# A delta-rule attention and two-MoE kernel: 32-row inverse steps on VectorE and GpSimd for the first two units, and a reordered start

## The chip, the cores and the metric

The kernel runs on 1 core of one Trainium2 chip. The metric is the device time of one execution in microseconds (us), lower is better. The engines are TensorE (PE in the profile; its weight loads are PEld), VectorE (DVE), ScalarE (ACT), GpSimd (POOL) and SyncE (SP), which issues most DMAs.

## The reference

Three stages follow each other. The first is a delta-rule attention over 4 x 8 heads, 768 tokens, head dimension 48; its output is laid out as 3072 tokens of 384 numbers. The second is a mixture of 8 experts of width 1024 whose weights P come from a softmax-like matrix that is normalised 8 times by rows and columns. The third is a dense layer of width 2048 with h * cos(h) in the middle.

```python
k_n = k / (norm(k) + 1e-06)
for t in range(S):
    y[:, :, t] = q[:, :, t] @ state
    v_old = k_n[:, :, t] @ state
    state = state + beta[t] * outer(k_n[:, :, t], v[:, :, t] - v_old)
...
logits = x @ w_gate; P = exp(logits - logits.max())
for _ in range(8):
    P /= P.sum(1) + 1e-09; P /= P.sum(0) + 1e-09; P *= N / E
for e in range(E):
    out += P[:, e:e + 1] * (maximum(x @ w1[e], 0.0) @ w2[e])
...
h = x @ w_in
return (h * cos(h)) @ w_out
```

## The kernel before, in words

The attention runs in 12 units of 64 tokens (C = 64), each split into two blocks of 32 (CB = 32). A unit holds all 32 heads as 16 systems side by side (NS = 16) in 4 groups of 32 partitions. Inside a block the recurrence is a unit lower triangular system, and the kernel inverts it: N is the triangular matrix of key products times beta (tiles n0 and ns0 of the buffer scr for units 0 and 1, Nst and Nsys for two units at a time later), transposed by VectorE so that each system lies in one partition as 32 x 32. The inverse is then built by a ladder of steps j: a product (row j of the result times column j) into a temporary, and an addition into all rows below j. Each step needs the one before it.

- For units 2 and 3 and later pairs the ladder (inv_ops, lines 388 and 392) runs on GpSimd over 32 rows: 30 steps of two instructions. It starts with the transpose into Nsys on VectorE (L374) and an affine_select on GpSimd (L377) into Xsys, a part of the buffer w1t.
- For units 0 and 1 the ladder (inv16, lines 408 and 409) runs on VectorE as two 16-row blocks at once: 14 steps of two instructions, on data whose upper triangles have been set to zero by a product with the mask m16 (L824). The off-diagonal 16 x 16 block is made on TensorE afterwards by merge16_a (L418), a scaling on VectorE (L427) and merge16_b (L437), then added by merge16_c (L444) and transposed (L447).
- The inverse comes out in two orientations, tiles tx and dm. pe_Z1 (L463) and pe_Z2 (L475) combine the two 32-token blocks of a unit into the tile Bs; pe_U multiplies it with the values (L526), and VectorE takes the product out of PSUM into U (L532). pe_S (L541, L546) updates the state, pe_PU (L556) and pe_XT (L573) make the unit's output.

The order of the work at the start is written out by hand, call by call, under manual_schedule, and each engine executes its instructions in that order. The string SEQ follows: its letters are read by tick (U pe_U, S pe_S, P pe_PU, K and k the products with the state, Z or Y and z or y the two halves of Bs, X the output transpose, H the first expert's first matmuls (L139), m half a step of the first expert, a and b the splitting of its weights, r and R the transposes of the later inverse into dm and tx). From H on, the expert matmuls of L139 and L150 are mixed in between the attention units, and then follow the other experts and the last layer.

The tick function calls inv_some(3) before every letter, which takes up to three queued ladder steps; before the change the queue is already empty when SEQ starts, since inv_some(99) has issued all of it to GpSimd.

norm_a and norm_b compute key norms for a pair of units, norm_pe (L783) swaps them across partitions on TensorE, beta_raw (L791, L795) folds them into beta, and n_dve (L807, then a product on GpSimd, L345) completes N for units 2 and 3. go_beta (L771) scales the tile Go that pe_Z1 reads, v_scale (L239) scales V, and pp_mask (L829) masks the tile Pp on GpSimd.

Of the kernel before, what the change touches and what calls it, by code (L numbers as in the profile page):

```python
# [11 lines left out]
ALU = mybir.AluOpType  # L12
# [13 lines left out]
SEQ = ("U0 a0 y1 o2 S0 x1 b0 P0 K1 o3 k1 v U1 X0 P1 S1 X1 H0 x2",  # L26
# [12 lines left out]
def kernel(  # L39
# [133 lines left out]
    m16 = ap1.tile([128, CB], F32, name="m16")  # L173
# [4 lines left out]
    betam = ap1.tile([128, 2, NS], F32, name="betam")  # L178
# [193 lines left out]
    def inv_ops(nst, nsys, xsys, tmp, eng):  # L372

        ops = [lambda: nc.vector.transpose(out=nsys, in_=nst.rearrange("p s t -> p t s"))]  # L374

        def first():
            nc.gpsimd.affine_select(  # L377
                out=xsys, in_=nsys, pattern=[[1, CB], [-1, CB]], compare_op=ALU.is_gt, fill=0.0, base=0,
                channel_multiplier=0,
            )  # L380
            nc.gpsimd.memset(xsys.rearrange("p t i -> p (t i)")[:, 0:CB * CB:CB + 1], 1.0)

        ops.append(first)
# [12 lines left out]
        return ops


    def inv16(xsys, tmp):
# [4 lines left out]
        def step(j):
            n = 15 - j
            a = tmp[:, 0:2 * n * j].rearrange("p (a t i) -> p a t i", a=2, t=n)
            x = blk(j + 1, 0, CB, 1, n, j)
            nc.vector.tensor_tensor(out=a, in0=blk(j + 1, j, CB, 0, n, j), in1=blk(j, 0, 0, 1, n, j), op=ALU.mult)
            nc.vector.tensor_tensor(out=x, in0=x, in1=a, op=ALU.add)

        return [lambda j=j: step(j) for j in range(1, 15)]

    def merge16_a(u, n, bank, y=True):

# [7 lines left out]
        if y:  # L422
            merge16_y(u, bank)

    def merge16_y(u, bank):
        ym[u] = ap2.tile([128, NS, CB], F32, tag="W", name="ym")
        nc.vector.tensor_tensor(  # L427
            out=ym[u][:, :, 0:16], in0=bank[:, 0:NS * 16].rearrange("p (s t) -> p s t", t=16),
            in1=betam[:, u, :, None].to_broadcast([128, NS, 16]), op=ALU.mult,
        )  # L430

    def merge16_b(u, bank, s0=0, s1=NS):
        y = ym[u]
        for s in range(s0, s1):
            for p in range(4):
                r = slice(p * CB, p * CB + CB)
                nc.tensor.matmul(  # L437
                    out=bank[r, (NS + s) * 16:(NS + s + 1) * 16], lhsT=dm[r, u * NS + s, :], rhs=y[r, s, 0:16],
                    start=True, stop=True, skip_group_check=True,
                )  # L440
# [8 lines left out]
    ym = {}  # L449
# [20 lines left out]
    def pe_Z2(u, bank=pcd[:, 1]):  # L470
# [8 lines left out]
        if u not in Bs:  # L479
            bs_act(u)  # L480
# [8 lines left out]
    def bs_act(u):  # L489
        x = tx[:, (u % 2) * NS:(u % 2 + 1) * NS, :]  # L490
        Bs[u] = ap2.tile([128, NS, C], F32, tag="Bs", name="Bs", bufs=1)
        for a in range(2):
            nc.scalar.activation(out=Bs[u][:, :, a * CB:a * CB + CB], in_=x, func=ACTF.Copy, scale=hm[:, a:a + 1])
# [204 lines left out]
    with tc.manual_schedule():  # L698
# [34 lines left out]
        nc.gpsimd.memset(m16, 1.0)  # L733
        nc.gpsimd.memset(hm, 0.0)
        for r in range(4):
            m = m16[r * CB:(r + 1) * CB]
            nc.gpsimd.affine_select(
                out=m, in_=m, pattern=[[1, CB]], compare_op=ALU.is_gt, fill=0.0, base=0, channel_multiplier=-1
            )
            nc.gpsimd.memset(m[0:16, 16:CB], 0.0)  # L740
# [3 lines left out]
            nc.gpsimd.memset(h_[0:16, 4:5], 1.0)  # L744
# [11 lines left out]
        inv_q = []  # L756

# [30 lines left out]
        def beta_raw(u0, bank):  # L788
# [6 lines left out]
            nc.vector.tensor_copy(out=dv[:, u0:u0 + 2, :].rearrange("p u (m i) -> p u m i", i=2), in_=x[:, 1])  # L795
# [62 lines left out]
        nc.vector.transpose(out=ns0, in_=xs0.rearrange("p s t -> p t s"))  # L858
# [11 lines left out]
        for u in range(2):  # L870
            nc.scalar.activation(
                out=betam[:, u].rearrange("p (i m) -> p i m", i=2),
                in_=beta_sb[:, u, 0:NS].rearrange("p (m i) -> p i m", i=2), func=ACTF.Copy, scale=hm[:, 4:5],
            )
# [7 lines left out]
        n_act(3, p23)  # L882
        pe_GQ_mms(1, p01)
# [61 lines left out]
        def tick(u, seq):  # L945
            early = u < 2
            for x, c in enumerate(seq.split()):
# [983 lines left out]
```

## Time and profile before

| what | value |
|---|---|
| median of 3 runs | 2084.89 us (2082.3 to 2086.13) |
| the profiled execution | 2088.02 us |
| its span, first to last instruction | 2085.9 us |
| PE busy | 2053.4 us, 98% of the span |
| PEld busy | 1729.9 us, 83% |
| DVE busy | 1461.4 us, 70% |
| ACT busy | 866.1 us, 42% |
| POOL busy | 905.7 us, 43% |
| mean granted TensorE clock | 0.987 |

Busy times are of one profiled execution; the shares of the engines overlap. An engine's busy share is an average over stages with different limits, so the stage that a change touches has to be read by itself: here the first hundred microseconds.

### The profile page before, as it was taken

What the parts mean: (1) busy time and instruction counts of PE and PEld (TensorE: products, weight loads), DVE (VectorE), ACT (ScalarE), POOL (GpSimd) and SP (SyncE); (2) the same over time, 40 slices, a digit from 0 to 9 for tenths busy, and PEclk for the clock granted to TensorE, in tenths of its full rate; (3) what the DMA queues carried; (4) which work ended last, traced back from release to release, by engine and by line L of the source; (5) the groups of instructions that cost most, each with busy time, mean ns of one, the idle gap of its engine ahead of it and who ended that gap; (6) DMA issues with size and microseconds to landing.
All of it is one profiled execution on the core that took longest, in us unless ns stands there. A gap on an engine that the chain in (4) does not pass through costs nothing.

```text
span 2085.9 us, 39694 instructions
## 1 busy us (share of the span) xinstructions
PE 2053.4 (98%) x16132; PEld 1729.9 (83%) x16132; DVE 1461.4 (70%) x2253; ACT 866.1 (42%) x1436; POOL 905.7 (43%) x1012
## 2 busy tenths in 40 slices
PE   7999999999999999999999999999999999999999
PEld 6887888778888888888888888888888889999998
DVE  6665537677677777777767787787788666666665
ACT  3442333344444444434333333333333356666664
POOL 4676660156555655544353333333333343333331
PEclk7899999999999999999999999999999999999999
DMA  5532346765554544453684544535354551011000
GB/s 94 127 94 57 78 127 196 296 237 164 193 172 157 204 169 169 177 179 136 249 302 143 173 151 142 173 120 192 130 174 144 185 201 31 1 31 31 16 16 15
DMA packets 212470, 294.39 MB, mean 141 GB/s; under 512 B 86160, under 2 KB 159344, under 8 KB 212288
## 3 DMA queue, kind: packets, MB, share of 16 engines
q1 hardware_dynamic: 208368, 284.20, 41.3%
q0 software_dynamic: 1664, 6.49, 0.9%
q8 instruction: 126, 2.06, 0.4%
q10 hardware_dynamic: 2256, 1.18, 0.2%
q14 instruction: 56, 0.46, 0.1%
HBM read 188.95 MB, written 113.87 MB: 145 GB/s over the span
## 4 chain that ended last, share of the span: by engine, by line
PE 91%; POOL 3%; DVE 2%; SPq 1%; issue 1%; DMA 1%; ACT 1%; ACTq 0%; POOLq 0%; DVEq 0%
PE ps L150 36%; PE ps L1469 27%; PE ps L1759 10%; PE ps L1717 9%; PE ps L139 4%; PE ps L313 1%; POOL w1t L392 1%; POOL w1t L388 1%; PE ps L498 1%; PE ps L281 1%; PE ps L526 1%; PE ps L463 0%; PE ps L556 0%; PE ps L475 0%; PE ps L573 0%
## 5 line engine op out<-in xcount | busy, mean ns | idle before, releaser
L150 PE MATMUL ps<-mh,w2t 128*128 128x512 f32 x3060 | 749.3, 389 | 0.4 <-DVE cth L1505 0.4
L150 PEld LDWEIGHTS ps<-mh,w2t 128*128 128x128 f32 x3060 | 573.5, 188 | 122.0 <-DVE cth L1505 3.3
L1469 PE MATMUL ps<-T,w1t 128*128 128x512 f32 x2520 | 627.2, 389 | 1.9 <-ACT ct L1474 0.8
L1506 POOL TENSOR_TENSOR accp<-accp,cth 128x512 f32<-128x512 f32 x246 | 320.3, 1333 | 562.8 <-DVE cth L1505 562.8
L1469 PEld LDWEIGHTS ps<-T,w1t 128*128 128x128 f32 x2520 | 472.2, 188 | 101.6 <-ACT ct L1474 1.3
L156 ACT ACTIVATE mh<-ps 128x512 fp32r<-128x512 f32 x340 | 203.6, 600 | 620.7 <-PE ps L1469 237.3
L157 DVE SCALAR_TENSOR_TENSOR mh<-ps,mh 128x512 fp32r<-128x512 f32 x340 | 228.8, 688 | 176.8 <-ACT mh L156 175.4
L1474 ACT ACTIVATE scr<-ps 128x512 f32<-128x512 f32 x224 | 134.5, 600 | 163.7 <-PE ps L1469 154.4
L1726 POOL TENSOR_SCALAR tp<-tp 128x512 f32<-128x512 f32 x92 | 91.5, 994 | 204.2 <-ACT tp L1725 204.2
L1505 DVE TENSOR_TENSOR cth<-ps,scr 128x512 f32<-128x512 f32 x246 | 154.3, 684 | 15.2 <-PE ps L150 13.3
L1740 DVE TENSOR_TENSOR tp<-tp,ps 128x512 f32<-128x512 f32 x96 | 66.1, 688 | 133.5 <-ACT tp L1739 133.5
L1477 DVE TENSOR_TENSOR ps<-scr,ps 128x512 f32<-128x512 f32 x168 | 116.5, 694 | 54.6 <-PE ps L1469 53.1
L139 PE MATMUL ps<-xb,w1t 128*128 128x512 f32 (+1 forms) x441 | 111.4, 397 | 0.0
L150 PE MATMUL ps<-h,w2t 128*128 128x512 f32 x396 | 100.8, 400 | 0.0
L1477 DVE TENSOR_TENSOR scr<-ps,scr 128x512 f32<-128x512 f32 x112 | 77.1, 689 | 30.5 <-PE ps L1469 29.2
L139 PEld LDWEIGHTS ps<-xb,w1t 128*128 128x128 f32 x441 | 78.6, 188 | 17.1 <-DVE xb L579 0.9
L1309 DVE TENSOR_TENSOR w1t<-wraw,w1t 128x512 fp32r<-128x512 f32 (+2 forms) x81 | 74.7, 934 | 19.1 <-ACT w1t L1306 17.9
L150 PEld LDWEIGHTS ps<-h,w2t 128*128 128x128 f32 x396 | 73.4, 190 | 15.7 <-issue 0.2
L392 POOL TENSOR_TENSOR w1t<-w1t 128x30 f32<-128x30 f32 (+9 forms) x150 | 80.7, 538 | 11.7
L1717 PE MATMUL ps<-xx,cw 128*128 128x512 f32 x360 | 84.0, 390 | 0.0
L388 POOL TENSOR_TENSOR w1t<-Nsys,w1t 128x30 f32<-128x30 f32 (+9 forms) x150 | 77.9, 520 | 11.4
L1725 ACT ACTIVATE tp<-ps 128x512 f32<-128x512 f32 x96 | 56.2, 586 | 63.5 <-PE ps L1717 63.5
(286 smaller groups left out, 2769.2 us busy)
## 6 DMA issues: line engine op xcount, KB each, us to landing
wss<-w1t SPq DMA_DIRECT2D x56, 768.0 KB
w1t<-wss SPq DMA_DIRECT2D x56, 768.0 KB
w2t<-w2c SPq DMA_DIRECT2D x56, 384.0 KB
T<-tsc SPq DMA_DIRECT2D x22, 512.0 KB
scr<-pts SPq DMA_DIRECT2D x44, 256.0 KB
w2c<-in_moe_w_dram SPq DMA_DIRECT2D x28, 384.0 KB
wss<-w1t SPq DMA_DIRECT2D x28, 384.0 KB
w1t<-wss SPq DMA_DIRECT2D x28, 384.0 KB
```

The lines of the kernel that those rows point to most:

```text
L139: nc.tensor.matmul(out=ps[:, :nn], lhsT=w[:, a, kk, fs], rhs=x[:, b, kk, c0:c0 + nn], start=(i == 0), stop=(i == 3 * KD - 1),)
L150: nc.tensor.matmul(out=banks[kd], lhsT=w[:, a, f % 2, kd * 128:(kd + 1) * 128], rhs=h[:, b, :], start=(first and b == 0 and a == 0), stop= ...
L156: nc.scalar.activation(out=h[:, 0, :nn], in_=ps[:, :nn], func=ACTF.Relu)
L157: nc.vector.scalar_tensor_tensor(out=h[:, 1, :nn], in0=ps[:, :nn], scalar=0.0, in1=h[:, 0, :nn].bitcast(F32), op0=ALU.max, op1=ALU.subtract,)
L392: eng.tensor_tensor(out=xsys[:, j + 1:, 0:j], in0=xsys[:, j + 1:, 0:j], in1=a, op=ALU.add)
L1469: nc.tensor.matmul(out=bank, lhsT=s_of(n, nm, a), rhs=T[:, b, :], start=start and q == 0, stop=q == 2, skip_group_check=True)
L1474: nc.scalar.activation(out=out, in_=in_, func=ACTF.Copy, scale=scale)
L1477: nc.vector.tensor_tensor(out=out, in0=a, in1=b, op=op)
L1505: nc.vector.tensor_tensor(out=c, in0=yb[kd], in1=pslot[t], op=ALU.mult)
L1506: nc.gpsimd.tensor_tensor(out=a[:, kd, :], in0=a[:, kd, :], in1=c, op=ALU.add)
L1717: nc.tensor.matmul(out=hb2(i), lhsT=net_w1(f, a, kk), rhs=x2[b](c, kk), start=(j == 0), stop=(j == 3 * KD - 1))
L1759: nc.tensor.matmul(out=ybk[t][:, :DM], lhsT=h[:, a, ts], rhs=net_w2(f, c), start=(f == 0 and j == 0), stop=(f == FT2 - 1 and j == 2),)
```

## The change

Units 0 and 1 get a 32-row ladder that is split over two engines. VectorE runs steps 1 to 15 on columns 0 to 15 of all rows (step 15 only on rows 16 to 23), GpSimd runs the 16-row ladder of the lower right block and step 15 on rows 24 to 31. What was above the diagonal is cleared by 12 memsets on GpSimd (upper_zero) in place of the products with m16, and one of the two TensorE passes of the merge goes away. Scalings by beta and the mask of Pp for unit 1 move to GpSimd (go_beta, pp_mask); norms and the products of units 2 and 3 keep their place relative to them. Further, inv_ops gets an argument last: from step 22 on the steps of the first later pair (units 2 and 3) are issued to VectorE. Of the 32 queued operations all but 8 are issued at the start, and the last 8 wait in inv_last until letter r. pe_U(0), pe_Z1(1) and pe_S(0) move from SEQ into the start.

```diff
-SEQ = ("U0 a0 y1 o2 S0 x1 b0 P0 K1 o3 k1 v U1 X0 P1 S1 X1 H0 x2",
+SEQ = ("P0 y1 a0 x1 K1 b0 o2 k1 o3 v U1 X0 P1 S1 X1 H0 x2",
...
-    def inv_ops(nst, nsys, xsys, tmp, eng):
+    def inv_ops(nst, nsys, xsys, tmp, eng, last=CB):
...
         def mul(j):
             n = CB - 1 - j
+            e = nc.vector if j >= last else eng
             a = tmp[:, 0:n * j].rearrange("p (t i) -> p t i", t=n)
-            eng.tensor_tensor(
+            e.tensor_tensor(
...
-        return [lambda j=j: step(j) for j in range(1, 15)]
+        for j in range(1, 16):
+            step(nc.vector, 0, 0, j, tmp[:, 0:256], 0, CB if j < 15 else 24)
+        for j in range(1, 15):
+            step(nc.gpsimd, 16, 16, j, tmp[:, 256:512])
+        step(nc.gpsimd, 0, 0, 15, tmp[:, 256:512], 24)
...
+        def upper_zero(x, eng):
+            f = x.rearrange("p t i -> p (t i)")
+            eng.memset(f[:, 1:CB * CB:66], 0.0)
+            for r in range(2):
+                for c in range(2):
+                    eng.memset(f[:, 2 + 32 * r + c:CB * CB:132], 0.0)
+            for w in (4, 8, 16):
+                for t in range(0, CB, 2 * w):
+                    eng.memset(x[:, t:t + w, t + w:t + 2 * w], 0.0)
...
+        pp_raw(1, xs0.rearrange("p a c -> p (a c)").rearrange("p (s c) -> p s c", c=C), p01)
+        upper_zero(ns0, nc.gpsimd)
+        inv16(ns0, W0.rearrange("p s t -> p (s t)"))
+        nc.gpsimd.memset(n0[:, :, 16:CB], 0.0)
+        go_beta(0, nc.gpsimd)
+        go_beta(1, nc.gpsimd)
         v_scale(0, nc.gpsimd)
         pp_mask(0)
-        for x in inv16(ns0, W0.rearrange("p s t -> p (s t)")):
-            x()
-        inv_tx(ns0)
-        inv_dm(ns0)
+        pp_mask(1)
+        inv16_dm(ns0, n0)
+        inv16_tx(ns0, 16)
+        inv16_tx(ns0, 0)
+        merge16_b(0, n0, pab[:, 0])
         norm_red(2)
         norm_red(3)
         norm_a(2, 4)
+        merge16_c(0, pab[:, 0])
+        bs_act(0, 0)
+        merge16_b(1, n0, pab[:, 1])
         norm_b(2, 4)
         norm_sqr(2)
...
+        pe_Z1(0, p01[:, 0])
+        bs_act(0, 1)
         norm_pe(2, pab[:, 0])
+        nc.vector.transpose(out=beta_x, in_=bw[1].rearrange("p (u t) -> p u t", t=CB))
+        beta_raw_x(0)
         beta_raw(2, pab[:, 0])
         n_dve(2, pcd)
         n_dve(3, p23)
...
+        pe_KS(0)
+        pe_Z2(0, p01[:, 1])
         merge16_c(1, pab[:, 1])
-        pe_Z1(1, pab[:, 1])
...
+        inv_q.extend(inv_ops(Nst, Nsys, Xsys, tmp, nc.gpsimd, 22))
+        inv_some(len(inv_q) - 8)
+        inv_last.extend(inv_q)
+        inv_q.clear()
+        pe_U(0)
+        load_v(2)
+        pe_Z1(1, p01[:, 0])
+        pe_S(0)
+        load_k(5)
...
                 elif c == "r" and u + 1 < NU:
                     inv_some(99)
+                    while inv_last:
+                        inv_last.pop(0)()
                     inv_dm(Xsys)
```

VectorE's instructions around the first take-out of U: before, from the second merge16_c to the take-out (scr is the masked Pp, w1t in L129 an expert's weights).

```order
L444 TENSOR_TENSOR tx<-tx,ps_154 128x16x16
L447 STREAM_TRANSPOSE dm<-tx 128x512
L818 TENSOR_TENSOR scr_192<-ps_154,mask 128x1024
L916 STREAM_TRANSPOSE beta_x<-bw 128x384
L481 SCALAR_TENSOR_TENSOR Bs<-ps_154,hm,Bs 128x16x32
L799 TENSOR_TENSOR beta_x<-beta_x,nrm 128x2x16
L532 TENSOR_TENSOR U<-ps_154,beta_x 128x2x8x48
L129 TENSOR_TENSOR w1t<-stg,w1t 128x768
```

And with the change (w1t in L389 and L393 is Xsys, the inverse of units 2 and 3; L529 is the take-out of U).

```order
L812 SCALAR_TENSOR_TENSOR w2t<-ps_154,hm,w2t 128x512 x2
L478 SCALAR_TENSOR_TENSOR Bs<-ps_154,hm,Bs 128x16x32
L430 SCALAR_TENSOR_TENSOR tx<-tx,hm,ps_154 128x16x16
L434 STREAM_TRANSPOSE dm<-tx 128x512
L374 STREAM_TRANSPOSE Nsys<-w2t 128x1024
L389 TENSOR_TENSOR w1t<-Nsys,w1t 128x198
L393 TENSOR_TENSOR w1t<-w1t 128x9x22
L529 TENSOR_TENSOR U<-ps_154,beta_x 128x2x8x48
L543 TENSOR_TENSOR S_185<-S_184,ps_154 128x2x2x192
```

The transpose into Nsys and both instructions of step 22 (9 rows by 22 columns) now stand ahead of the take-out of U on VectorE.

GpSimd with the change, from the end of its own 16-row ladder to the first steps of the later ladder (Go, v, Pp and scr are the scalings and masks; L345 completes N of units 2 and 3).

```order
L407 TENSOR_TENSOR W_193<-scr_192 128x120
L411 TENSOR_TENSOR scr_192<-scr_192,W_193 128x8x15
L894 MEMSET scr_192 128x32x16
L765 TENSOR_TENSOR Go<-Go,beta_sb 128x512 x2
L239 TENSOR_TENSOR v<-v,dv 128x768
L838 TENSOR_TENSOR Pp<-Pp,mask 128x1024
L838 TENSOR_TENSOR scr_192<-scr_192,mask 128x1024
L345 TENSOR_TENSOR w2t<-w2t,beta_sb 128x512 x2
L377 AFFINE_SELECT w1t<-Nsys 128x1024
L381 MEMSET w1t 128x32
L389 TENSOR_TENSOR w1t<-Nsys,w1t 128x30
L393 TENSOR_TENSOR w1t<-w1t 128x30
```

Before the change, of these only v, one Pp and what follows stood there; both Go products were VectorE's.

## Rows read from the trace of the kernel before

**Rows 1.** The page: busy time of each engine over the whole span.

```profile
PE 2053.4 (98%) x16132; PEld 1729.9 (83%) x16132; DVE 1461.4 (70%) x2253; ACT 866.1 (42%) x1436; POOL 905.7 (43%) x1012
```

**Rows 2.** Windows: start:end and length, busy per engine, PEclk, DMA share, GB/s.

```profile
40.00:50.00 10.00, 7.45 (x368) 6.97 (x368) 7.36 (x12) 1.94 (x3) 5.70 (x12) 0.50 0.28 48
...
80.00:90.00 10.00, 10.00 (x143) 8.22 (x135) 7.22 (x15) 3.77 (x7) 4.71 (x12) 1.00 0.87 203
```

**Rows 3.** Timeline of PE: start, length, engine, line, op, out<-in, count [idle before].

```profile
35.20 1.90 PE L418 MATMUL ps<-tx,scr 32*32 32x16 f32 x128 [1.37 <-issue]
...
39.54 0.64 PE L783 MATMUL ps<-nrm,ident 128*128 128x32 f32 x2
...
74.48 2.75 PE L139 MATMUL ps<-xb,w1t 128*128 128x256 f32 x18
```

**Rows 4.** Timeline of VectorE, 14 to 57 us.

```profile
14.03 0.69 DVE L824 TENSOR_TENSOR scr<-scr,m 128x512 f32<-128x512 f32 x1
...
18.25 1.96 DVE L858 STREAM_TRANSPOSE scr<-scr 128x1024 f32<-128x1024 f32 x1
20.28 0.17 DVE L408 TENSOR_TENSOR W<-scr 128x28 f32<-128x28 f32 x1
...
24.16 0.27 DVE L408 TENSOR_TENSOR W<-scr 128x112 f32<-128x112 f32 x1
...
27.81 0.19 DVE L409 TENSOR_TENSOR scr<-scr,W 128x28 f32<-128x28 f32 x1
...
31.64 1.78 DVE L235 TENSOR_REDUCE nrm<-sq 128x16 f32<-128x768 f32 x2
...
33.98 0.18 DVE L256 TENSOR_SCALAR nrm<-nrm 128x32 f32<-128x32 f32 x1 [0.30 <-ACT nrm L255]
...
35.65 0.19 DVE L779 TENSOR_TENSOR nrm<-nrm 128x32 f32<-128x32 f32 x1
...
47.65 0.71 DVE L447 STREAM_TRANSPOSE dm<-tx 128x512 f32<-128x512 f32 x1
...
53.05 0.75 DVE L481 SCALAR_TENSOR_TENSOR Bs<-ps,hm,Bs 128x512 f32<-128x512 f32 x1 [3.10 <-PE ps L475]
...
56.20 0.96 DVE L532 TENSOR_TENSOR U<-ps,beta_x 128x768 f32<-128x768 f32 x1 [2.30 <-PE ps L526]
```

**Rows 5.** Timeline of GpSimd, 29 to 75 us.

```profile
29.86 1.48 POOL L239 TENSOR_TENSOR v<-v,dv 128x768 f32<-128x768 f32 x1 [16.05 <-DMA v<-in_v_dram]
31.30 2.35 POOL L829 TENSOR_TENSOR Pp<-Pp,mask 128x1024 f32<-128x1024 f32 x1
41.67 2.07 POOL L345 TENSOR_TENSOR w2t<-w2t,beta_sb 128x512 f32<-128x512 f32 x2 [8.02 <-DVE w2t L807]
45.76 1.27 POOL L377 TENSOR_SCALAR_AFFINE_SELECT w1t<-Nsys 128x1024 f32<-128x1024 f32 x1 [2.02 <-DVE Nsys L374]
...
47.17 0.25 POOL L388 TENSOR_TENSOR w1t<-Nsys,w1t 128x30 f32<-128x30 f32 x1
...
57.66 1.18 POOL L388 TENSOR_TENSOR w1t<-Nsys,w1t 128x220 f32<-128x220 f32 x1
...
74.89 0.54 POOL L388 TENSOR_TENSOR w1t<-Nsys,w1t 128x198 f32<-128x198 f32 x1
```

**Rows 6.** Timeline of GpSimd in the second later ladder, 119 to 121 us.

```profile
119.11 0.56 POOL L388 TENSOR_TENSOR w1t<-Nsys,w1t 128x198 f32<-128x198 f32 x1
...
120.41 0.61 POOL L388 TENSOR_TENSOR w1t<-Nsys,w1t 128x210 f32<-128x210 f32 x1
```

**Rows 7.** Timeline of VectorE beside it.

```profile
119.25 0.46 DVE L256 TENSOR_SCALAR nrm<-nrm 128x16 f32<-128x16 f32 x1
...
120.40 0.18 DVE L259 TENSOR_TENSOR nrm<-nrm 128x16 f32<-128x16 f32 x1
```

**Rows 8.** Timelines of VectorE and PE at letter r, after the expert's start.

```profile
90.41 2.07 DVE L452 STREAM_TRANSPOSE dm<-w1t 128x1024 f32<-128x1024 f32 x1
...
95.56 1.20 PE L463 MATMUL ps<-dm,Go 32*32 32x32 f32 x64
```

More of the change, by code (lines that the diff above doesn't have):

```diff
@@ L172 @@
     mask = ap1.tile([128, C], F32, name="mask")
-    m16 = ap1.tile([128, CB], F32, name="m16")
+    ap1.tile([128, CB], F32, name="pad4")
     dv = ap1.tile([128, 4, NS], F32, name="dv")
@@ L421, in merge16_a, with inv16_dm, inv16_tx @@
                 )
[L422 to L440, printed above, removed]
     def merge16_c(u, bank):
         x = tx[:, u * NS:(u + 1) * NS, 16:32]
-        nc.vector.tensor_tensor(
-            out=x, in0=x, in1=bank[:, NS * 16:2 * NS * 16].rearrange("p (s t) -> p s t", t=16), op=ALU.add
+        nc.vector.scalar_tensor_tensor(
+            out=x, in0=x, scalar=hm[:, 4:5], in1=bank[:, 0:NS * 16].rearrange("p (s t) -> p s t", t=16),
+            op0=ALU.mult, op1=ALU.add,
         )
         nc.vector.transpose(out=dm[:, u * NS:(u + 1) * NS, :], in_=tx[:, u * NS:(u + 1) * NS, :])
-    ym = {}
+    def inv16_dm(xsys, n):
+        nc.vector.transpose(
+            out=dm.rearrange("p s j -> p j s")[:, 0:16], in_=xsys.rearrange("p t j -> p j t")[:, 0:16]
+        )
+        for u in range(2):
+            s = slice(u * NS, (u + 1) * NS)
+            nc.scalar.activation(out=n[:, s, 0:16], in_=dm[:, s, 0:16], func=ACTF.Copy, scale=hm[:, 4:5])
+    def inv16_tx(xsys, t):
+        nc.vector.transpose(out=tx.rearrange("p s t -> p t s")[:, t:t + 16], in_=xsys[:, t:t + 16])
     def inv_dm(xsys):
@@ L487, with bs_act @@
     Bs = {}
[L489 removed]
+    def bs_act(u, a):
         x = tx[:, (u % 2) * NS:(u % 2 + 1) * NS, :]
[L491 to L493 removed]
+        if a == 0:
+            Bs[u] = ap2.tile([128, NS, C], F32, tag="Bs", name="Bs", bufs=1)
+        nc.scalar.activation(out=Bs[u][:, :, a * CB:a * CB + CB], in_=x, func=ACTF.Copy, scale=hm[:, a:a + 1])
     def state_mms(bank, t, u, keys, more=False):
@@ L756 @@
         inv_q = []
+        inv_last = []
         def inv_some(n):
@@ L786, in norm_pe, with beta_raw_b @@
                 )
-        def beta_raw(u0, bank):
+        def beta_raw_b(u0, bank):
             x = bank[:, 0:64].rearrange("p (i f u m) -> p f u m i", i=2, f=2, u=2)
@@ L794, in beta_raw, with beta_raw_d @@
             )
-            nc.vector.tensor_copy(out=dv[:, u0:u0 + 2, :].rearrange("p u (m i) -> p u m i", i=2), in_=x[:, 1])
+        def beta_raw_d(u0, bank, eng=nc.vector):
+            x = bank[:, 0:64].rearrange("p (i f u m) -> p f u m i", i=2, f=2, u=2)
+            o = dv[:, u0:u0 + 2, :].rearrange("p u (m i) -> p u m i", i=2)
+            if eng is nc.vector:
+                eng.tensor_copy(out=o, in_=x[:, 1])
+            else:
+                eng.activation(out=o, in_=x[:, 1], func=ACTF.Copy)
+        def beta_raw(u0, bank):
+            beta_raw_b(u0, bank)
+            beta_raw_d(u0, bank)
         def beta_raw_x(u0):
@@ L845 @@
         gk_n(0, pcd, n0)
+        norm_sqr(0)
+        norm_pe(0, p01[:, 0])
         pe_T(kr[2], pab)
-        norm_raw(0, p01[:, 0])
-        m16_mul(0)
+        nc.vector.transpose(out=beta_sb, in_=bw[0].rearrange("p (u t) -> p u t", t=CB))
         gk_n(1, p23, n0)
-        m16_mul(1)
-        nc.vector.transpose(out=beta_sb, in_=bw[0].rearrange("p (u t) -> p u t", t=CB))
-        beta_raw(0, p01[:, 0])
+        beta_raw_b(0, p01[:, 0])
         for u in range(2):
-            gk_b(u, xs0[:, u * NS:(u + 1) * NS, :], nc.vector)
+            gk_b(u, n0[:, u * NS:(u + 1) * NS, :], nc.vector)
         raw(0, pcd)
@@ L857 @@
         raw(1, p23)
-        nc.vector.transpose(out=ns0, in_=xs0.rearrange("p s t -> p t s"))
+        beta_raw_d(0, p01[:, 0], nc.scalar)
+        nc.vector.transpose(out=ns0, in_=n0.rearrange("p s t -> p t s"))
         nc.vector.memset(ns0.rearrange("p t i -> p (t i)")[:, 0:CB * CB:CB + 1], 1.0)
@@ L869 @@
         n_act(2, pcd)
[L870 to L874, printed above, removed]
+        raw(2, pcd)
         norm_sq(2, "D")
```

62 lines of the change are left out of this document (19 added, 43 removed).

## The prediction

> **What bounds the kernel now.** I read the page's busy times first, then windows, then the timelines of the first hundred microseconds, then single rows for prices. TensorE is busy for 2053.4 us of 2085.9 [rows 1], so 32.5 us are all that it ever idles. The windows show where: between 40 and 50 us it works 7.45 us of 10, and at a granted clock of 0.50, its level of 1.2 GHz; between 80 and 90 it works all 10 us at 1.00, 2.4 GHz [rows 2]. So the kernel has two regimes. From the first expert matmul on, at 74.48 [rows 3], TensorE is full, and other engines matter only if they make it wait. Ahead of 74.48 it waits for a chain through all engines. Whatever moves 74.48 moves the end by the same amount. The change works in that first part, so its price is the shift of 74.48, plus what it disturbs shortly after.
>
> In the chain the step to watch is VectorE's take-out of U for unit 0, at 56.20 [rows 4]. The state update, everything of unit 1 and the expert's input follow it. From 56.20 to 74.48 are 18.28 us.
>
> **The wait that the change adds.** In the new order VectorE has the transpose into Nsys and both instructions of step 22 of the later ladder ahead of the take-out of U. VectorE executes in order, and step 22 reads what step 21 has written, on GpSimd. So U cannot be taken out before GpSimd has done 21 steps. Before, VectorE had no part in that ladder and took U out while GpSimd was in it: the ladder's first step began at 47.17 and step 22 at 74.89 [rows 5]. Queued on VectorE behind the wait are U, the state update S, the second Bs, the expert's weights and D of unit 1; TensorE waits for U to make S, and has nothing else, since the expert's input is unit 0's own output. One might read the constants (from step 22, all but 8 operations at the start) as leaving only steps 23 to 30 for later and nothing of VectorE's at the start; but the queue holds 32 operations of which 30 are steps, so the last 8 are steps 23 to 30, and step 22 is in. Hence the time of U is the sum below.
>
> **When the units 0, 1 ladders end.** The two products with m16 go (0.69 each [rows 4]), so the transpose into ns0 starts about 1.3 us ahead of its 18.25, and ends at 18.95. For VectorE's ladder the old one gives two constants: from 20.28 to 28.00 it ran 28 instructions over 2240 elements, and an instruction of 112 elements took 0.27, one of 28 took 0.19 [rows 4], or 0.95 ns an element; what is left is 0.20 us an instruction. The new one has 30 instructions over 4720 elements (sums of the order's widths): 6.0 + 4.5 = 10.5, so it ends at 29.5 alone. GpSimd first has 12 small memsets, 1.2 us by an estimate of 0.1 each. Its price per step comes from the later ladder: 42 instructions over 7700 elements from 47.17 to 74.89, 27.7 us [rows 5]. Three of them lasted about 1.2 us where their like last 0.6 (the one at 57.66 [rows 5]; the 0.61 of 210 elements [rows 6]), an excess of 1.75, so 26.0 undisturbed; at 1.7 ns an element (0.25 at 30, 0.54 at 198 [rows 5]) that is 0.30 an instruction. The new 28 instructions over 1120 elements: 8.4 + 1.9, and two of 120: 1.0. Together 18.95 + 1.2 + 10.3 + 1.0 = 31.5.
>
> Do the two ladders hinder each other? A VectorE instruction of 16 elements that began at 119.25, inside a GpSimd instruction of 119.11 to 119.67, lasted 0.46 and ended just behind it; one that began at 120.40, together with a GpSimd instruction of 0.61, lasted 0.18 and neither was longer [rows 6, 7]. So they exclude each other, but for the streaming part of an instruction and not for what lies around it. The floor is 0. The ceiling is a full exchange, 28 times the 0.2 us that VectorE's instructions have besides their elements, about +6. I take +1, nearest the row with 0.18, since GpSimd's steps here stream only 14 to 56 elements: both ladders have ended at E = 32.5.
>
> The Trainium skill, SBUF — State Buffer, section "Who interferes with whom", says that a VectorE instruction with two SBUF inputs and a GpSimd one that reads SBUF share a port pair, and that the first to issue holds it "for the whole instruction". By that the ladders would end some 5 us later, and the sum would be +29 instead of +24; the row with 0.18 speaks against the letter of it, the row with 0.46 for it.
>
> **From E to the take-out of U**, in us behind E:
> - VectorE: three transposes of 512 elements at 0.71 and two reductions, 1.78: 3.9; norm_a, merge16_c (0.2 and 0.4 by the constants above) and its transpose 0.71: 5.3 [rows 4]. TensorE's merge of unit 0, 128 records in 1.90 [rows 3], lies beside the reductions.
> - norm_b and the square behind it took 33.98 to 35.84, 1.86 us [rows 4]. But GpSimd now does a memset (0.5), two Go products (2.07 for two of the same shape), v 1.48 and two masks at 2.35 [rows 5]: 8.8 us. By the exclusion above, VectorE's two-input steps fall behind these long instructions, and I put their end at 10.1 (7.2 if nothing were excluded).
> - norm_pe on TensorE, beta_raw, n_dve and the products on GpSimd: before from 39.54 [rows 3] to 43.74, the end of the two L345 [rows 5], 4.2 us: 14.3.
> - Meanwhile Z2 has followed norm_pe on TensorE; behind n_dve VectorE has Bs 0.75, merge16_c 0.42 and its transpose 0.71 [rows 4]: 15.1. The transpose into Nsys, 1.96 at its size [rows 4]: 17.0.
> - affine_select and memset up to the first step: 45.76 to 47.17 [rows 5], and a hand-over of 0.1: 18.5.
> - 21 steps on GpSimd: 26.0, since VectorE stands still and cannot hinder it: 44.5.
> - step 22 on VectorE, two instructions of 198 elements at 0.39: 45.3.
>
> So U is taken out at 32.5 + 45.3 = 77.8 in place of 56.20: **+21.6**.
>
> **From there to the expert.** The same work follows; the second Z2, which ran beside the take-out of U before, now lies behind S and PU (+1.9), and Z1 and a fetch gap are out of the way: I take +0.5. The 256 merge records that go (3.8 us at 1.90 per 128 [rows 3]) end no wait here, nor do the moved evictions on ScalarE, which lie inside the stall; DMAs keep their order, and the load of V waits for unit 0's product with Bs, which is still done in the stall.
>
> **At letter r**, 16 ladder instructions over 1824 elements now stand on VectorE ahead of the transpose into dm: 16 x 0.20 + 1.7 = 4.9 us. Before, that transpose ran 90.41 to 92.48, and TensorE's Z1, which reads it, began at 95.56 [rows 8]: 3.1 us of slack. Z1 comes 1.8 us late, and VectorE is nearly full there: +2 (0 to 5).
>
> **Sum:** 21.6 + 0.5 + 2 = +24.1. The profiled execution took 2088.0, its span 2085.9; so 2112.1 for one like it. The median shown is 3.1 lower, and I put the forecast on the median: **2109.0**. A measurement of this kernel tells about 0.2%, 4 us, from no change.
>
> **Rivals.**
> 1. *The ladders exchange the port instruction by instruction*, and the masks too. E moves to about 38, the time to 2114 to 2120. For it: the 0.46 and the 1.18 [rows 5, 7]. Against: the 0.18 [rows 7]. The page named above states it. 0.15.
> 2. *Part is paid back.* GpSimd and VectorE do not meet in the prologue (E = 30.5 with memsets of next to nothing, norm_b at 7.2), TensorE, waking behind the stall with work for many microseconds, gets its 2.4 GHz sooner relative to the expert (up to 2 us), and r costs nothing: 24.1 - 2 - 2.9 - 2 - 2.5 = +14.7, 2099.6; with GpSimd's steps a little shorter 2098. 0.13.
> 3. *The wait does not bind*: VectorE reaches step 22 when GpSimd is through step 21. Then U is ready when TensorE's product is (14.0 for Bs and 2.3 as in the wait of the take-out [rows 4]), E + 16.3 = 48.8, 7.4 us sooner, and 2084.9 - 7.4 + 2.5 = 2080. The point that decides: GpSimd's 21 steps must have begun by 22 us, ahead of the end of the ladder that feeds beta; only a chip that runs these steps several times faster than 0.6 us each does that. Faster: 0.04.
> 4. *Both effects cancel*, a shorter way to U and a shorter stall: within 0.2%. 0.02.
>
> The forecast, 2104 to 2114, has 0.66. Slower by over 0.2% are forecast and rivals 1 and 2: 0.94. **Range** 2098 to 2120: the low end from rival 2, the high end from rival 1 (+5.5, with +5 at r in place of +2, and GpSimd's steps at 27.7 in place of 26.0).
>
> **What would show it.** Right: U's take-out near 78 with step 22 just before it, VectorE idle for some 26 us released by GpSimd's ladder, TensorE idle as long, the first expert matmul near 97, 16 ladder instructions on VectorE ahead of dm at r. Wrong: U before 60, or VectorE's idle time under 10 us; for rival 1, ladder instructions of 0.4 us and more on VectorE and E near 38.

## The result, and the profile after

The change is slower: 2114.24 us median (2111.95 to 2117.18, 4 runs) against 2083.6 (2080.54 to 2086.13, 4 runs), a ratio of 1.0148, 95% interval 1.0126 to 1.0171. That is 30.6 us more; 24.1 were forecast. 2114.24 lies inside the stated 2098 to 2120, but 0.2 above the narrower 2104 to 2114 that the forecast itself was given, and at the low end of what rival 1 said, 2114 to 2120. So the time alone does not tell the forecast from rival 1; the trace has to. The profiled execution of the change took 2117.18 us, 29.2 more than the profiled one of before (2088.02).

The page of the change shows TensorE with almost the same work in a longer span; it answers to [rows 1].

```profile
span 2115.5 us, 39224 instructions
...
PE 2049.2 (97%) x15876; PEld 1725.2 (82%) x15876; DVE 1463.8 (69%) x2266; ACT 866.4 (41%) x1440; POOL 907.1 (43%) x1035
```

PE's busy time is 4.2 us less (256 merge matmuls went, 3.8 us by [rows 3]), while the span is 29.6 longer: TensorE stands still for longer. The windows of the change say where (columns as in [rows 2]).

```profile
52.00:56.00 4.00, 0.00 (x0) 0.00 (x0) 0.00 (x0) 0.00 (x0) 3.37 (x9) 0.50 0.45 89
...
72.00:76.00 4.00, 0.00 (x0) 0.00 (x0) 0.00 (x0) 0.00 (x0) 3.53 (x7) 0.50 0.00 0
...
116.00:120.00 4.00, 2.23 (x10) 1.50 (x8) 3.73 (x10) 0.00 (x0) 0.00 (x0) 1.00 0.00 0
120.00:124.00 4.00, 2.29 (x128) 2.14 (x128) 3.46 (x9) 3.04 (x6) 1.53 (x1) 0.87 0.01 4
124.00:128.00 4.00, 2.81 (x11) 2.65 (x12) 4.00 (x4) 1.02 (x2) 2.77 (x2) 0.50 0.32 105
```

From 52 to 76 us no engine but GpSimd computes anything. A second, smaller hole lies at 116 to 128, where TensorE is at work about 60% of the time and its granted clock falls from 1.00 to 0.50, from 2.4 to 1.2 GHz. VectorE's timeline of the change names what it stood for in the first hole (it answers to [rows 4]).

```profile
30.30 0.28 DVE L411 TENSOR_TENSOR scr<-scr,W 128x120 f32<-128x120 f32 x1
...
36.48 1.72 DVE L248 TENSOR_SCALAR nrm<-nrm 128x32 f32<-128x32 f32 x1
...
39.49 1.01 DVE L256 TENSOR_SCALAR nrm<-nrm 128x32 f32<-128x32 f32 x1
...
41.98 0.19 DVE L773 TENSOR_TENSOR nrm<-nrm 128x32 f32<-128x32 f32 x1
...
47.06 1.89 DVE L374 STREAM_TRANSPOSE Nsys<-w2t 128x1024 f32<-128x1024 f32 x1
76.10 0.36 DVE L389 TENSOR_TENSOR w1t<-Nsys,w1t 128x198 f32<-128x198 f32 x1 [27.15 <-POOL w1t L393]
76.50 0.36 DVE L393 TENSOR_TENSOR w1t<-w1t 128x198 f32<-128x198 f32 x1
76.78 0.95 DVE L529 TENSOR_TENSOR U<-ps,beta_x 128x768 f32<-128x768 f32 x1
```

Step 22 of the later ladder waited 27.15 us, released by GpSimd's additions, and the take-out of U stood right behind it, at 76.78 in place of 56.20. GpSimd's timeline of the change (it answers to [rows 5]):

```profile
31.51 0.42 POOL L411 TENSOR_TENSOR scr<-scr,W 128x120 f32<-128x120 f32 x1
...
35.81 2.35 POOL L838 TENSOR_TENSOR Pp<-Pp,mask 128x1024 f32<-128x1024 f32 x1
38.11 2.35 POOL L838 TENSOR_TENSOR scr<-scr,mask 128x1024 f32<-128x1024 f32 x1
44.35 2.07 POOL L345 TENSOR_TENSOR w2t<-w2t,beta_sb 128x512 f32<-128x512 f32 x2 [3.88 <-DVE w2t L812]
...
50.44 0.25 POOL L389 TENSOR_TENSOR w1t<-Nsys,w1t 128x30 f32<-128x30 f32 x1
...
75.48 0.58 POOL L393 TENSOR_TENSOR w1t<-w1t 128x210 f32<-128x210 f32 x1
```

TensorE's timeline of the change (it answers to [rows 3, 8]):

```profile
77.79 1.53 PE L538 MATMUL ps<-U,kr 64*48 64x48 f32 x64 [27.55 <-DVE U L529]
...
96.14 3.70 PE L139 MATMUL ps<-xb,w1t 128*128 128x256 f32 x18
...
113.86 2.33 PE L139 MATMUL ps<-xb,w1t 128*128 128x512 f32 x9
...
120.05 1.20 PE L459 MATMUL ps<-dm,Go 32*32 32x32 f32 x64 [1.82 <-DVE dm L448]
121.18 1.16 PE L313 MATMUL ps<-KT 48*64 48x64 f32 x64
125.19 1.94 PE L281 MATMUL ps<-ident,kr 128*128 128x128 f32 x8 [2.85 <-DVE kr L265]
126.78 3.73 PE L139 MATMUL ps<-xb,w1t 128*128 128x512 f32 x9
...
132.66 2.34 PE L150 MATMUL ps<-h,w2t 128*128 128x512 f32 x9
```

And the kernel before, for the rows at 113.86 and from 125.19 on:

```profile
91.26 2.33 PE L139 MATMUL ps<-xb,w1t 128*128 128x512 f32 x9
...
97.90 1.06 PE L281 MATMUL ps<-ident,kr 128*128 128x128 f32 x8
98.72 2.30 PE L139 MATMUL ps<-xb,w1t 128*128 128x512 f32 x9
...
103.18 2.33 PE L150 MATMUL ps<-h,w2t 128*128 128x512 f32 x9
```

The first expert matmul is 21.7 us late (96.14 against 74.48). At the half-step ahead of r the delay is 22.6 (113.86 against 91.26; the first matmuls, in part at 1.2 GHz, took 3.70 in place of 2.75), and behind r it is 29.5 (132.66 against 103.18). So r cost 6.9 us: two waits of TensorE, 1.82 for dm and 2.85 for the scaled keys, then a transpose of 1.94 in place of 1.06 and matmuls of 3.73 in place of 2.30 at the lower clock, together 7.0. Behind that nothing is lost or won: the span is 29.6 longer.

Why the scaled keys came late shows in L265, the instruction on VectorE that scales them. First the kernel before:

```profile
95.21 2.46 DVE L265 TENSOR_TENSOR kr<-kr,nrm 128x768 f32<-128x768 f32 x1
```

Then the change, VectorE and GpSimd:

```profile
122.64 2.45 DVE L265 TENSOR_TENSOR kr<-kr,nrm 128x768 f32<-128x768 f32 x1
```

```profile
122.47 1.80 POOL L129 TENSOR_TENSOR w1t<-stg,w1t 128x768 fp32r<-128x768 f32 x1 [46.40 <-ACT w1t L128]
```

In both kernels L265 lasts about 2.46, where the same instruction for the keys of the unit ahead took 0.96; in both it begins 0.16 or 0.17 us behind GpSimd's product L129, and so it does in every run below. In the kernel before its end, 97.67, was only just in time for TensorE's transposes at 97.90. In the change it ended at 125.09 and they began at 125.19.

### The profile page after: what moved, and what is told of

It reads as the page before. It is cut to its first block, busy times and chain, and to the rows that moved or that the text cites. A ratio compares the mean times of both kernels' runs of the same rounds, so it can differ in the third digit from the quotient of the medians.

```text
span 2115.5 us, 39224 instructions
## 1 busy us (share of the span) xinstructions
PE 2049.2 (97%) x15876; PEld 1725.2 (82%) x15876; DVE 1463.8 (69%) x2266; ACT 866.4 (41%) x1440; POOL 907.1 (43%) x1035
## 3 DMA queue, kind: packets, MB, share of 16 engines
q10 hardware_dynamic: 2256, 1.18, 0.2%
## 4 chain that ended last, share of the span: by engine, by line
PE 89%; POOL 4%; DVE 4%; issue 1%; SPq 1%; DMA 1%; ACT 1%; ACTq 0%; POOLq 0%; DVEq 0%
PE ps L150 35%; PE ps L1484 26%; PE ps L1774 9%; PE ps L1732 9%; PE ps L139 4%; POOL w1t L393 1%; POOL w1t L389 1%; PE ps L313 1%; PE ps L495 1%; PE ps L471 1%; PE ps L281 1%; PE ps L553 0%; PE ps L459 0%; PE ps L538 0%; PE ps L523 0%
## 5 line engine op out<-in xcount | busy, mean ns | idle before, releaser
L157 DVE SCALAR_TENSOR_TENSOR mh<-ps,mh 128x512 fp32r<-128x512 f32 x340 | 228.2, 686 | 177.4 <-ACT mh L156 175.9
L1520 DVE TENSOR_TENSOR cth<-ps,scr 128x512 f32<-128x512 f32 x246 | 154.1, 681 | 15.7 <-PE ps L150 13.3
L1492 DVE TENSOR_TENSOR scr<-ps,scr 128x512 f32<-128x512 f32 x112 | 76.9, 687 | 31.1 <-PE ps L1484 30.2
L1324 DVE TENSOR_TENSOR w1t<-wraw,w1t 128x512 fp32r<-128x512 f32 (+2 forms) x81 | 76.0, 952 | 18.5 <-ACT w1t L1321 17.2
L150 PEld LDWEIGHTS ps<-h,w2t 128*128 128x128 f32 x396 | 73.5, 190 | 15.7
L393 POOL TENSOR_TENSOR w1t<-w1t 128x30 f32<-128x30 f32 (+9 forms) x141 | 74.6, 529 | 11.1
L1293 POOL TENSOR_TENSOR w2t<-w2t 128x768 fp32r<-128x768 f32 x28 | 55.2, 1972 | 55.4 <-ACT w2t L1289 55.4
```

The costliest lines, as they stand in the source:

```text
L150: nc.tensor.matmul(out=banks[kd], lhsT=w[:, a, f % 2, kd * 128:(kd + 1) * 128], rhs=h[:, b, :], start=(first and b == 0 and a == 0), stop= ...
L157: nc.vector.scalar_tensor_tensor(out=h[:, 1, :nn], in0=ps[:, :nn], scalar=0.0, in1=h[:, 0, :nn].bitcast(F32), op0=ALU.max, op1=ALU.subtract,)
L393: e.tensor_tensor(out=xsys[:, j + 1:, 0:j], in0=xsys[:, j + 1:, 0:j], in1=a, op=ALU.add)
L1492: nc.vector.tensor_tensor(out=out, in0=a, in1=b, op=op)
L1520: nc.vector.tensor_tensor(out=c, in0=yb[kd], in1=pslot[t], op=ALU.mult)
```

## The experiments

Two theories stood against each other. Theory S, the prediction's: VectorE's in-order wait for GpSimd's step 21 holds U, and with it everything. Theory R: the new start itself is long, by the port that VectorE and GpSimd share and by the masks, and step 22 only stands where it shows.

The runs below start from the kernel with the whole change unless they say otherwise; each time is set against the kernel before, run beside it.

**Step 22 late.** Nine steps in place of eight are left for r.

```diff
-        inv_some(len(inv_q) - 8)
+        inv_some(len(inv_q) - 9)
```

> Step 22 goes with steps 23 to 30 to letter r; nothing else changes. Theory S (VectorE's in-order wait for GpSimd's step 21 is what holds U): U is taken out near 48.5 instead of 76.8, the first expert matmul comes near 68 instead of 96, and VectorE has 18 ladder instructions at r (5.7 us), which costs TensorE 5 to 9 us there; time 2084 to 2091. Theory R (the new start itself is long, by the shared port and the masks, and step 22 only stands where it shows): U no earlier than 60, time above 2098.

2088.64 us (11 runs) against 2085.06 for the kernel before; ratio 1.0024 (1.0015 to 1.0033). One instruction pair placed elsewhere makes the change 25.6 us faster (27.0 if each is set against its own runs of before: 30.6 and 3.6 us), so theory R is out as the cause. VectorE's timeline of this run, and below it TensorE's at r:

```profile
48.87 0.92 DVE L529 TENSOR_TENSOR U<-ps,beta_x 128x768 f32<-128x768 f32 x1
```

```profile
90.77 1.92 PE L459 MATMUL ps<-dm,Go 32*32 32x32 f32 x64 [3.00 <-DVE dm L448]
...
95.91 1.94 PE L281 MATMUL ps<-ident,kr 128*128 128x128 f32 x8 [1.31 <-ACT w2t L338]
```

U comes at 48.87, 28 us sooner than in the change and 7.3 sooner than before, and the first expert matmul at 66.63. Yet the lead over the kernel before, 7.9 us there, is gone behind r, which costs 8.3 us: TensorE waits 3.00 for dm and 1.31 more ahead of the transposes, and its next matmuls take 3.94 in place of 2.30. (A lead read from two single executions is rough: with this same start the first expert matmul came between 66.63 and 69.97 in the five runs that have it, and with the start of before between 70.86 and 74.48 in three.) This run also shows what VectorE's standstill was worth to GpSimd: the 21 steps that took 25.6 us in the change took 30.2 here (50.43 to 80.66), beside a VectorE at work.

**All later steps on GpSimd.** The new start with the ladder as it was before.

```diff
-        inv_q.extend(inv_ops(Nst, Nsys, Xsys, tmp, nc.gpsimd, 22))
-        inv_some(len(inv_q) - 8)
+        inv_q.extend(inv_ops(Nst, Nsys, Xsys, tmp, nc.gpsimd))
+        inv_some(99)
```

> The whole later ladder is GpSimd's and is issued at the start, as in the kernel before; the rest of the change stays. Theory S: U near 48.5, expert near 68, and then r, which is reached about 16 us after the expert's start, near 83 to 84, waits for GpSimd's step 30 until about 90 (ladder from 50.4, some 38 to 40 us): 3 to 7 us lost there against a start that is 6 to 7 us ahead; time 2080 to 2087. Theory R: as for the run before, above 2098.

2089.58 us (8 runs), ratio 1.0025 (1.0015 to 1.0035). U and the expert came as expected (48.89, 68.23), and r waited for GpSimd as expected, but the loss at r was 8.1 us, where 3 to 7 had been allowed for (6.2 ahead of before at the half-step, 85.02 against 91.26, and 1.9 behind it after r, 105.05 against 103.18), so the time missed its range. VectorE's row at r:

```profile
90.28 1.91 DVE L448 STREAM_TRANSPOSE dm<-w1t 128x1024 f32<-128x1024 f32 x1 [5.65 <-POOL w1t L393]
```

The later ladder begins near 50 here and at 47.17 before [rows 5], so its result is not there sooner, however soon U is. The lead at the expert runs into it.

**Only step 22 on VectorE.** The wait ahead of U stays, steps 23 to 30 go to GpSimd at once.

```diff
-            e = nc.vector if j >= last else eng
+            e = nc.vector if j == last else eng
...
-        inv_some(len(inv_q) - 8)
+        inv_some(99)
```

> Step 22 stays on VectorE ahead of U, steps 23 to 30 go to GpSimd at once, so that nothing of the ladder is left for r. Theory S: U at 76.8 and the expert at 96 as in the change, no wait of TensorE at r and no drop of its clock there; time 5 to 8 us under the change, 2106 to 2109. If the time after the expert's start was lost to something else than the 16 instructions at r, it stays at 2112 to 2116.

2106.37 us (4 runs), ratio 1.0107 (1.0093 to 1.0121): 7.9 us under the change, or 9.3 by each one's own runs of before (30.6 and 21.3). Its timeline of TensorE keeps the long wait and has none at r:

```profile
79.29 1.53 PE L538 MATMUL ps<-U,kr 64*48 64x48 f32 x64 [27.03 <-DVE U L529]
...
116.50 1.20 PE L459 MATMUL ps<-dm,Go 32*32 32x32 f32 x64
...
118.72 1.09 PE L281 MATMUL ps<-ident,kr 128*128 128x128 f32 x8
```

So the 30.6 us are two separate losses: about 21 ahead of the expert (its first matmul began at 95.41 here, 74.48 before) and some 7 to 9 at r.

**GpSimd through step 25.** VectorE keeps steps 26 to 30 for r.

```diff
-        inv_q.extend(inv_ops(Nst, Nsys, Xsys, tmp, nc.gpsimd, 22))
-        inv_some(len(inv_q) - 8)
+        inv_q.extend(inv_ops(Nst, Nsys, Xsys, tmp, nc.gpsimd, 26))
+        inv_some(len(inv_q) - 5)
```

> GpSimd does steps 1 to 25 at once, VectorE does 26 to 30 (10 instructions, 2.8 us) at r. Theory S: U near 48.5, expert near 68, GpSimd through step 25 by 82, before r; the 2.8 us at r are under the 3.1 us of slack that Z1 had in the kernel before: time 2076 to 2081, under the kernel before. If the split at r costs by itself (any ladder work on VectorE there), 2082 or more.

2087.64 us (11 runs), ratio 1.0013 (1.0004 to 1.0021): a miss. Dm was in time, but TensorE still waited 1.03 and 1.54 us ahead of the transposes of the scaled keys and then ran its next matmuls in 3.33. The profile puts the first of these waits down to no other engine ("issue"); the second is the keys':

```profile
97.48 1.78 PE L281 MATMUL ps<-ident,kr 128*128 128x128 f32 x8 [1.54 <-DVE kr L265]
```

The slack of 3.1 us was that of dm alone.

**The part alone, in the kernel before.** Step 22 on VectorE at the start, steps 23 to 30 at r; the rest is the kernel before. Here step 22 stands ahead of the second merge16_c and not right ahead of U, which needs what follows from it. The edit of inv_ops itself, which gives it the argument last, is that of the change and is left out below, as is the line that makes the list inv_last.

```diff
-        inv_q.extend(inv_ops(Nst, Nsys, Xsys, tmp, nc.gpsimd))
+        inv_q.extend(inv_ops(Nst, Nsys, Xsys, tmp, nc.gpsimd, 22))
...
-        inv_some(99)
+        inv_some(len(inv_q) - 8)
+        inv_last.extend(inv_q)
+        inv_q.clear()
```

> The kernel before with one part of the change alone: step 22 on VectorE at the start (here ahead of the second merge16_c), steps 23 to 30 on VectorE at r. Theory S: VectorE stands still until GpSimd's step 21, near 73 (47.2 + 26.0); then merge16_c, Z1, Z2, Bs and unit 0's product follow, so U is taken out near 82 in place of 56 and the first expert matmul comes near 100; with some 7 us at r the time is 2112 to 2122, as slow as the whole change. Theory R (the new start is what is long): a part of the loss only, under 2100.

2114.22 us (4 runs), ratio 1.0137 (1.0123 to 1.0151): this one part, the wait and the tail at r together, makes the kernel before as slow as the whole change. VectorE's timeline:

```profile
72.41 0.37 DVE L389 TENSOR_TENSOR w1t<-Nsys,w1t 128x198 f32<-128x198 f32 x1 [26.09 <-POOL w1t L393]
...
80.79 0.96 DVE L533 TENSOR_TENSOR U<-ps,beta_x 128x768 f32<-128x768 f32 x1 [2.08 <-PE ps L527]
```

**The masks later.** As the run with GpSimd through step 25 (its two lines are not repeated below), with unit 0's mask behind the products of units 2 and 3, and unit 1's on VectorE.

```diff
         v_scale(0, nc.gpsimd)
-        pp_mask(0)
-        pp_mask(1)
...
         n_dve(3, p23)
+        pp_mask(0)
...
         pe_S(0)
+        pp_mask(1, nc.vector)
```

> As the run with GpSimd through step 25, and the two masks of Pp leave the place ahead of norm_a and norm_b: unit 0's goes behind the products of units 2 and 3 on GpSimd, unit 1's to VectorE behind the first state update. If GpSimd's long two-input instructions are what holds norm_a (1.72 in place of 0.2) and norm_b's first step (1.01), both are short, U is taken out 1 to 2 us sooner, near 46.5, and the later ladder starts no later than before; time 2082 to 2087, 1 to 4 us under that run. If VectorE's wait there was something else, both stay long and the time stays at 2086 to 2090.

2088.29 us (11 runs), ratio 1.0013 (1.0005 to 1.0022), a miss. The mechanism shows, the gain does not:

```profile
37.01 0.18 DVE L248 TENSOR_SCALAR nrm<-nrm 128x32 f32<-128x32 f32 x1
...
40.37 0.18 DVE L256 TENSOR_SCALAR nrm<-nrm 128x32 f32<-128x32 f32 x1
...
50.77 0.93 DVE L529 TENSOR_TENSOR U<-ps,beta_x 128x768 f32<-128x768 f32 x1
```

Both steps are at 0.18, where the change had 1.72 and 1.01, so GpSimd's masks did hold them. But U came at 50.77, later than the 48.04 of the run that it is built on: in this execution TensorE's transposes and key products ahead of the merge ran longer (1.98 for 64 key products, where the run with step 22 late has 1.16), and the merge began at 37.01 in place of 34.1. The later ladder, too, began later than in the change, at 52.34, and at r VectorE's step 26 waited 1.48 for GpSimd's step 25.

**The same with all later steps on GpSimd.**

```diff
-        inv_q.extend(inv_ops(Nst, Nsys, Xsys, tmp, nc.gpsimd, 26))
-        inv_some(len(inv_q) - 5)
+        inv_q.extend(inv_ops(Nst, Nsys, Xsys, tmp, nc.gpsimd))
+        inv_some(99)
```

> As the run before, with all 30 later steps on GpSimd at once. Theory S: r waits for GpSimd's step 30 (near 88) instead of doing 10 instructions itself; time within 2 us of the run before, 2082 to 2088.

2090.79 us (10 runs), ratio 1.0025 (1.0015 to 1.0034), 2.5 us above the run before it, and no better than the same without the masks moved. Yet this execution shows the gain that the one before it hid:

```profile
46.91 0.91 DVE L529 TENSOR_TENSOR U<-ps,beta_x 128x768 f32<-128x768 f32 x1
```

Counted from L437, the first transpose behind the ladders, U follows here after 15.7 us (31.18 to 46.91), and after 16.9 in all five runs in which the masks stay and U does not wait. So by this execution the masks cost the start 1.2 us. At r TensorE waits 3.64 for dm, and behind r the run is 1.2 us later than the profiled run of before (104.38 against 103.18). At its end it is 3.3 later; where the other 2 us went was not traced.

**VectorE's steps spread.** Built on the run with step 22 late; x is the place of a letter in its string.

```diff
                 inv_some(3)
+                if u == 2 and x in (6, 9):
+                    for _ in range(2):
+                        inv_last.pop(0)()
```

> As the run with step 22 late, but VectorE's nine steps are spread: 22 and 23 ahead of the second expert half-step's take-out, 24 and 25 ahead of the mask product of letter e, 26 to 30 at r. GpSimd is through step 21 by 77, when VectorE has idle time of its own. If it is the block of ladder instructions at r that costs, some 3 us of it fall into that idle time and the time is 2 to 4 us under that run, 2083 to 2087; if VectorE is full from the expert's start on and any added work there costs, it stays at 2087 to 2091.

2090.34 us (11 runs), ratio 1.0027 (1.0018 to 1.0035), no gain. Step 22 came to VectorE before GpSimd was through step 21 (at 80.62, not by 77 as expected), so the wait that the change had ahead of U stood, shorter, ahead of the half-step's take-out L157:

```profile
80.66 0.37 DVE L389 TENSOR_TENSOR w1t<-Nsys,w1t 128x198 f32<-128x198 f32 x1 [4.35 <-POOL w1t L393]
...
82.11 0.69 DVE L157 SCALAR_TENSOR_TENSOR h<-ps,h 128x512 fp32r<-128x512 f32 x1
```

TensorE then waited where it had not before: its second full group of expert matmuls began at 82.85 after 2.12 us of waiting for L157, and lasted 3.86 in place of 2.33. Of the 8.3 us that the run with step 22 late lost at r, some 3.7 came up here instead and 4.8 were still lost at r. So this run does not tell whether VectorE has room for the steps; it repeats the in-order wait in another place.

**The tail alone, in the kernel before.** As the part alone above, with 23 in place of 22 in its first line, so that no step of the ladder stands on VectorE ahead of U.

> The kernel before with the last part of the change alone: steps 23 to 30 on VectorE at r (16 instructions, 4.9 us), nothing ahead of U. By the prediction's term (the instructions less 3.1 us of slack) the loss is 2 us, 2086 to 2088; by what the change shows after its expert start (a wait for dm, then one for the scaled keys, then the lower clock) it is 5 to 8 us, 2090 to 2093.

2091.53 us (7 runs), ratio 1.0036 (1.0022 to 1.005): 6.3 us, three times the prediction's term. TensorE's timeline at r repeats the change's picture without its long wait:

```profile
94.57 1.20 PE L464 MATMUL ps<-dm,Go 32*32 32x32 f32 x64 [1.82 <-DVE dm L453]
...
99.71 1.94 PE L281 MATMUL ps<-ident,kr 128*128 128x128 f32 x8 [2.85 <-DVE kr L265]
101.30 3.60 PE L139 MATMUL ps<-xb,w1t 128*128 128x512 f32 x9
```

Set against the run of the part alone, 28.7 us over its own runs of before, this leaves 22.4 for the wait at the start.

**Letter w later**, in the run with GpSimd through step 25 and in the kernel before:

```diff
-        ... "r m M t O m w R m Z B t m z B i" ...
+        ... "r m M t O m R m w Z B t m z B i" ...
```

> As the run with GpSimd through step 25, and letter w (GpSimd's splitting of an expert's weights, 768 elements in two instructions) moves behind R and the next half-step. If the second wait at r is VectorE's key scaling (L265, 2.46 in place of 0.96) standing behind that GpSimd instruction, L265 lasts about 1, TensorE's transposes come 1.5 us sooner and its clock holds; time 2083 to 2086, 2 to 4 us under that run. If it is VectorE's lateness alone, 2086 to 2089.

> The kernel before with that one move of letter w. There the transposes wait for L265 with some 0.2 us to spare and TensorE loses nothing at r, so no gain: within 2 us of the kernel before, 2083 to 2087.

2087.88 us (ratio 1.0001, 0.9992 to 1.001) and 2085.92 us (ratio 0.999, 0.9981 to 0.9998), 11 runs each against 2087.88 for the kernel before, run beside them. The first settles nothing about the neighbour: GpSimd's weight product still began at 93.07 and VectorE's L265, at 93.24, still lasted 2.45. The move changed no engine's work there: in the timelines from 60 to 140 us ScalarE, VectorE and GpSimd execute the same instructions in the same order with and without it. GpSimd's product waits for ScalarE's L128, which stands behind L255 in ScalarE's order, and L255 waits for VectorE's own norms (L248); so the product is late whenever VectorE is late, and the two meet again. What L265 would cost without that neighbour was not tried in another way. Both runs are in effect repeats, and they say how far a ratio can be trusted: the same order read 1.0013 and 1.0001, and the kernel before against itself 0.999, with an interval that leaves out 1. Differences of 0.1% are not told apart here, and no version is faster than the kernel before by more than that.

## Why the prediction was right, and where it was short

Its steps against the trace of the change, E being the end of both ladders (rows three to six count from E):

| step | forecast | measured |
|---|---|---|
| E | 32.5 | 31.9 (31.51 + 0.42) |
| VectorE's ladder | 10.5 long, with no neighbour | 10.8, beside GpSimd's (19.79 to 30.58) |
| norms end | 10.1 | 10.2 (42.17) |
| products of units 2, 3 end | 14.3 | 14.5 (46.42) |
| first later step | 18.5 | 18.5 (50.44) |
| step 21 ends | 44.5 | 44.1 (76.06) |
| U taken out | 77.8 | 76.8 |
| from there to the expert | 18.8 | 19.4 (to 96.14) |
| at r | +2 | +6.9 |

- **The wait that the change adds** was the cause, shown from both sides: the change without it is 25.6 us faster, and the kernel before with that part alone, which holds the wait and the tail at r, is as slow as the change; of its 28.7 us the tail by itself makes 6.3. Reading the order, not the constants, decided it: with 30 steps among 32 queued operations, "all but 8" takes step 22 in, and the argument last gives it to VectorE.
- **Step 21's time.** 26.0 us for 21 undisturbed steps became 25.6 (50.44 to 76.06) with VectorE standing still, as the prediction had it; the rows of before, with a neighbour's disturbance, gave 27.7, and the run with step 22 late, with VectorE at work, 30.2.
- **The port.** The masks held norm_a for 1.72 and norm_b's first step for 1.01, and moving them brought both to 0.18. Rival 1, an exchange instruction by instruction, is out, although the measured time lies in its band: VectorE's ladder took 10.8 us beside GpSimd's, 10.5 was forecast without any neighbour, and E was 31.9 and not 38. The words "for the whole instruction" that the prediction quotes stand, in that section of the Trainium skill (SBUF — State Buffer, "Who interferes with whom"), with VectorE's two-port modes; of two-input instructions the section says that they contend with GpSimd's reads. Here long instructions did wait until the neighbour's end: of L265's 2.46 us in the kernel before, 0.80 lie behind the end of L129 at 96.87. The short ones of the ladders did not.
- **At r** is the term that was mis-sized. "Z1 comes 1.8 us late" was right (1.82 in the change and in the tail alone), but the prediction stopped at that first reader. VectorE stays 5 us late behind dm; the keys that it scales next had 0.2 us of slack before (L265 ended at 97.67, TensorE's transposes began at 97.90), not 3.1, and TensorE waited 2.85 more for them: 4.67 in all, which is the 4.9 of the instructions less this smaller slack. After the two holes its clock was at 1.2 GHz for some 5 us, another 2.3. The term measured 6.9 in the profile and 6.3 as a kernel of its own; with it in place of 2, the sum is 29.0, against 29.2 between the two profiled executions.
- **That this comes out so close is in part luck.** U came 20.6 later and not 21.6. The path from U to the expert grew by 1.1 and not by 0.5: TensorE's gap ahead of the last state products, which the profile puts down to issue, lasted 2.48 in place of 1.50, and no term had that. And the 0.9 by which the first expert matmuls were slower stood in no term.
- **Rival 2**, part paid back, did not come: E was 31.9 and not 30.5, the norms ended 10.2 behind it and not 7.2, the clock rose behind the stall (1.00 from 88 to 92 us) but fell again ahead of the expert (0.53 from 92 to 96, with a wait of 1.18 for U and the gap of 2.48), and r cost more, not nothing.
- **Rival 3**, no wait at all, has its price from the run with step 22 late: U was 7.3 us sooner than before, as the 7.4 there said. But its 2080 did not follow: 2088.64, with nine steps at r where rival 3 had eight. The lead is paid back at r, either by VectorE's own ladder steps or by the wait for GpSimd's.

## What to carry to other kernels

Before moving a step of a sequential chain to another engine, read in the engines' order what stands behind it there: an in-order engine hands its wait on to all that follows, and two instructions of 0.36 us cost about 22 us. When work is added to a nearly full engine, the slack to compare it with is the smallest among all readers of what that engine makes next, not that of the first. And a chain that begins earlier gains nothing beyond the next place where it meets a ladder that does not begin earlier.

## What the runs showed of the hardware that had not been expected

- In the two ladders side by side it was GpSimd whose instructions grew: its additions of 44 elements took 0.28 and later, beside longer instructions of VectorE, 0.37, while VectorE's of 228 to 238 elements took 0.40 to 0.41, no more than its price without a neighbour gives (0.42 to 0.43). In these rows of the change, GpSimd's (first fence) and VectorE's:

```profile
22.90 0.28 POOL L411 TENSOR_TENSOR scr<-scr,W 128x44 f32<-128x44 f32 x1
...
28.39 0.37 POOL L411 TENSOR_TENSOR scr<-scr,W 128x44 f32<-128x44 f32 x1
```

```profile
27.36 0.40 DVE L407 TENSOR_TENSOR W<-scr 128x228 f32<-128x228 f32 x1
```

- TensorE's clock costs more around a short hole than the hole itself suggests: at r, 4.7 us of waiting were followed by 2.3 us of slower work. And it fell at different moments of the start in different executions of nearly the same program: the 64 key products of about 28 us took 1.98 in the run with the masks later and 1.16 in the one with step 22 late, which shifted the merge by 3 us and hid what the masks gave. From U to the first expert matmul the same order took between 17.8 and 21.9 us in five executions; the traces show different clocks and different gaps put down to issue there, and the two were not separated.
